# Loading w4 by seven and wo by two neighbouring rows per partition, with w3, V and the gather's operand read in steps

## The chip, the cores and the metric

One core of a Trainium2 chip runs the whole program. Its engines are TensorE (PE; loads of the stationary operand are listed apart as PEld), VectorE (DVE), ScalarE (ACT), GpSimd (POOL) and SyncE (SP), which issues nearly all transfers; 16 DMA engines carry them. The metric is device time in microseconds (us), the median of several runs.

## The reference

Two layers, each an attention block and an MLP block, for eight rows (one token each) of width 448, in bf16:

```
x = x + A(layernorm(x));  x = x + B(layernorm(x));  x = x + A(layernorm(x));  x = x + B(layernorm(x))

A(x): q = x @ wq                       16 heads of 256; 8 K/V heads, each shared by two q heads
      p = softmax(q . k_cache / 16)    over 4096 cached positions per row and K/V head
      o = p . v_cache
      return o @ wo                    wo is 4096 x 448: row 256*head + d

B(x): (x is one token: the shifted branch of the reference adds zeros)
      h = gelu(layernorm(x) @ w3)      w3 is 448 x 1792
      return x + h @ w4                w4 is 1792 x 448
```

Both layers use the same weights and the same caches. k_cache and v_cache are 8 x 8 x 4096 x 256 bf16, 134 MB each. The kernel keeps some K between the layers and loads V twice.

## The kernel before, in words

**Tiles.** A K or V head of one row is 2 MB, cut into four blocks of 512 KB; a block fills one of 31 slots in SBUF (`slots`, `NSLOT`), 2048 bf16 on each of 128 partitions, which is eight neighbouring cache positions of 256. One transfer brings one, two or four blocks. wq, wo, w3 and w4 stay in SBUF. wo lies as 32 tiles of 128 rows x 448 (`wo_sb`), w4 as 14 such tiles (`w4_sb`): partition m of tile t holds row 128 t + m, so that a transfer takes 448 elements (896 B) at a time from DRAM. w3 lies with its 448 input features on partitions, as three tiles and a rest (`w3_sb`, `w3t_sb`).

**Attention.** K blocks are turned for the scores either by TensorE and ScalarE (`transpose`, evicted by a copy) or by VectorE in 32 x 32 squares (line 960, which writes to another slot). TensorE forms the scores (lines 948, 969, 997). For V there are two forms, in `vpart`:

- *still* (line 1111): a 128 x 128 piece of a V block is the stationary operand, and two columns of probabilities move. The output has the head's 256 features on partitions, as two columns `cc` of 128. A block takes 16 matmuls.
- otherwise (line 1137): the probabilities are stationary and V moves, 512 columns at a time. The sum over partitions of the result follows in `gather` (line 1159): ScalarE and VectorE copy the sum from PSUM into a slot as two bf16 parts, and pieces of 128 columns of it are the stationary operand of eight matmuls.

Both leave the attention output with 128 features of a head per column; `outproj` (1185) and `outproj8` (1200) multiply such a column with the wo tile of the same 128 features.

**The MLP.** `project` multiplies 128 columns of w3 (stationary) with the normed token, 14 times four matmuls (lines 588 and 590), into 14 columns of PSUM; `gelu` works on these; `down` multiplies column k with w4's tile k (line 613). All eight batch rows together pass through it once at the end (`end`), and each row alone passes between its two layers, in a *turn* (`turn`, `block`): output projection, norm, w3, gelu, w4, norm, and wq for layer 1. The last row passes the last MLP alone as well (`end1`). In `block` w3's product runs beside the reciprocal root of the norm's variance (lines 545 to 555 on VectorE, after a sum over partitions on GpSimd), and both meet in the scaling at line 675.

**Order.** `Plan.schedule` is a list scheduler that runs before the launch. It books each operation at a given cost and each transfer at its bytes divided by 410 (or 415) bytes per ns, one after the other. From this it settles the order of instructions on every engine, the slot of each block, and whether a transfer of two or four blocks is cut. SP issues the transfers in that order, each as soon as its slots are free. The byte counts of wo and w4 carry a factor of 1.1 in these bookings. wo's transfers are issued after ten transfers of the first K and V blocks, w4's after the first row's layer-0 blocks.

The loads of w3, wo and w4, before (lines 440, 449 and 450 of the kernel):

```
U_w3 = [rows(f"w3{k}", w3_sb[:, k, :], B_w3[k * P:(k + 1) * P, :], P * 3584) for k in range(3)]
...
U_wo = [rows(f"wo{i}", wo_sb[:, 8 * i:8 * i + 8, :], wo_src[:, 8 * i:8 * i + 8, :], P * 7168 * 1.1) for i in range(4)]
U_w4 = [rows("w4", w4_sb[:, :, :], B_w4.rearrange("(t m) n -> m t n", m=P), P * 12544 * 1.1)]
```

Of the kernel before, what the change touches and what calls it, by code (L numbers as in the profile page):

```python
# [3 lines left out]
P = 128  # L4
# [5 lines left out]
DH = 256  # L10
F = 1792
NCH = 4
# [348 lines left out]
def bass_interleave_layers__gqa_block_cached__mixer_s_mlp__decode_kernel(  # L361
# [83 lines left out]
        u.side = True  # L445
    U_even = [U_wq.pop(), U_w3.pop()]
    wq_rest, w3_rest = ([U_side[i], U_even[i]] for i in range(2))
    wo_src = A_wo.rearrange("(t m) n -> m t n", m=P)
    U_wo = [rows(f"wo{i}", wo_sb[:, 8 * i:8 * i + 8, :], wo_src[:, 8 * i:8 * i + 8, :], P * 7168 * 1.1) for i in range(4)]
    U_w4 = [rows("w4", w4_sb[:, :, :], B_w4.rearrange("(t m) n -> m t n", m=P), P * 12544 * 1.1)]  # L450

    def chunks(cache, b, h, name, skip=(), most=2):

# [123 lines left out]

        return j // 4 * 4 + j % 2 * 2 + j // 2 % 2

    def project(w, wt, half, j0, j1, rhs, out0, nb, units, bufs, name, place=lambda j: j):  # L580


        def emit(e):
            last = None
            for j in range(j0, j1):
                o = psT[:, out0 + place(j) * nb:out0 + (place(j) + 1) * nb]
                for k in range(3):
                    e.matmul(o, w[:, k, j * P:(j + 1) * P], rhs(0, P, k), start=(k == 0), stop=False)
                i, k = (j, 4) if j < half else (j - half, 3)
                last = e.matmul(o, wt[:, i * P:(i + 1) * P], rhs(0, P, k), start=False, stop=True)  # L590
            return last
        add("pe", emit, (j1 - j0) * 4 * 27, bufs, [], [bT], units, name=name, n=4 * (j1 - j0))

# [60 lines left out]
    def block(b, n, last, base):  # L654


        x = xT[:, :, b]
        dve(lambda e: e.memset(syn, 0.0), 125, [], [Bs["yn"]], name=n + "c0")
        dve(lambda e: e.memset(sx1[64:128, 4:5], 0.0), 125, [], [Bs["x4"]], name=n + "c1")
        dve(lambda e: e.tensor_reduce(sjk[:, :], psT[:, base:base + 24].rearrange("p (s c) -> p c s", c=4), axis=AX.X, op=ALU.add),  # L660
            180, [], [Bs["jk"]], [bT], name=n + "ao")
        dve(lambda e: e.tensor_tensor(sjk[:, :], sjk[:, :], x[:, 0:4], ALU.add), 150, [Bs["jk"], Bx[b]], [Bs["jk"]], name=n + "xa")
        outproj(*last, [0], base)
        dve(lambda e: e.tensor_tensor(sjk[:, :], psT[:, base + 24:base + 28], sjk[:, :], ALU.add), 150, [Bs["jk"]], [Bs["jk"]], [bT], name=n + "xb")
        plan.turn = not base
        outproj(*last, [1], base)
        dve(lambda e: e.tensor_tensor(sx1[:, 0:4], psT[:, base + 28:base + 32], sjk[:, :], ALU.add), 150, [Bs["jk"]], [Bs["x1"]], [bT], name=n + "x1")
        norm1(sx1[:, :], Bs["x1"], Bs["x4"], 40, n + "a")
        rhs = lambda p0, p1, k: syn[p0:p1, k, 1:2]
        project(w3_sb, w3t_sb, 7, 0, 14, rhs, 16, 1, U_w3 + w3_rest, [Bs["yn"]], n + "w3")  # L670
        root(lambda: sf[:, 5:6], lambda k: sf[:, (1, 6, 7, 8)[k]:(2, 7, 8, 9)[k]],
             (WEIGHT[0] / WEIGHT[1], WEIGHT[0] * (EPS[0] - EPS[1]), ALU.mult, ALU.add), [Bs["sq"]], [Bs["f1"]], [], n + "n1", True)
        dve(lambda e: e.scalar_tensor_tensor(sxy[:, :], sxc[:, 0:4], sf[:, 5:6], sx1[:, 0:4], ALU.mult, ALU.add),
            160, [Bs["xc"], Bs["f1"], Bs["x1"]], [Bs["xy"]], name=n + "xy")
        gelu(1, lambda: shf[:, :], lambda: sht[:, :], 16, [], n, 150, lambda e, o, i: e.tensor_single_scalar(o, i, sf[:, 2:3], ALU.mult), Bs["f"])
        down(1, lambda: sht[:, :], 32, [], n + "w4")
        dve(lambda e: e.scalar_tensor_tensor(x[:, 0:4], psT[:, 32:36], 0.5, sxy[:, :], ALU.mult, ALU.add), 150,
            [Bs["xy"]], [Bx[b]], [bT], name=n + "r2")
# [114 lines left out]
    def end():  # L793

        w = Wide(None, wq_sb[:, 0, 0:SLOT])
        u = []
        v3 = lambda a: a.rearrange("p (c b) -> p c b", b=B)
        x1, x3 = w.tile(bf, 40), w.tile(bf, 32)
        b1, by, b3 = Buf(), Buf(), Buf()
        ao, xy = w.tile(f32, 32), w.tile(f32, 32)  # L800
        bao = Buf()
        b1.readers = [r for u_ in U_wq for r in u_.readers]
        dve(lambda e: e.memset(x1()[64:128, 32:40], 0.0), 100, [], [b1], units=u, name="ex0")
        for m in range(HKV // 2):
            outproj8(m, m, plan.prio)
        dve(lambda e: e.tensor_reduce(ao(), psT[:, 0:256].rearrange("p (s c) -> p c s", c=32), axis=AX.X, op=ALU.add),
            450, [], [bao], [bT], units=u, name="eao")
        dve(lambda e: e.tensor_tensor(x1()[:, 0:32], ao(), xT[:, 0:4, :].rearrange("p c b -> p (c b)"), ALU.add), 200, [bao, b1] + Bx, [b1], units=u, name="ex1")
        u_, bu, yn, byn, roots = norm8(w, lambda: v3(x1()), [b1], 320, "e")
        rhs = lambda p0, p1, k: yn()[p0:p1, 8 * k:8 * k + 8]  # L810
        project(w3_sb, w3t_sb, 7, 0, 14, rhs, 32, 8, U_w3 + w3_rest + u, [byn], "ew3")
        mul, br = roots(True, "e")
        mul1, br1 = roots(False, "ey")
        dve(lambda e: mul1(e, xy(), u_()[:, 0:32]), 200, [bu, br1], [by], units=u, name="ey")
        dve(lambda e: e.tensor_tensor(xy(), xy(), x1()[:, 0:32], ALU.add), 200, [by, b1], [by], units=u, name="exy")
        ht, hf = w.tile(bf, 112), w.tile(f32, 112)
        Bg = {k: Buf() for k in ("ht", "hf")}
        gelu(8, hf, ht, 32, u, "e", 280, mul, br, Bg)
        down(8, ht, 160, u, "ew4", Bg)
        dve(lambda e: e.scalar_tensor_tensor(x3(), psT[:, 160:192], 0.5, xy(), ALU.mult, ALU.add), 200, [by], [b3], [bT], units=u, name="er2")  # L820

        def back(e):
            last = None
            for cc in (3, 0, 1, 2):
                d0 = cc * P if cc < 3 else D - P
                o = psT[0:B, 0:224].bitcast(bf)[:, d0:d0 + P]
                last = e.transpose(o, x3()[:, 8 * cc:8 * cc + 8], ident[:, :])
            return last
        add("pe", back, 400, [b3, Bc], [], [bT], u, name="eback")
        xo = w.tile(bf, D)  # L830
        bxo = Buf()
        dve(lambda e: e.tensor_copy(xo()[0:B, :], psT[0:B, 0:224].bitcast(bf)), 450, [], [bxo], [bT], units=u, name="exo")
        late.append(plan.load(Unit("out", lambda e, _: e.dma_start(out[0:B - 1, 0, :], xo()[0:B - 1, :]), 7168, slotted=False),
                              after=bxo.writers))
        return w
# [244 lines left out]
    def vpart(at, p, still, bank, most, aside):  # L1080
# [14 lines left out]
        if still:  # L1095
            for s in range(2):
                x = bank ^ s if layer else bank
                for c in range(NCH):
                    u = p.V[NCH * s + c]

                    def pv(e, u=u, c=c, s=s, x=x):

                        for cc in range(2):
                            o = psV[x][:, 4 * s + 2 * cc:4 * s + 2 * cc + 2]
                            for j in range(8):
                                i = j * DH + cc * P
                                if c < p.nns[s]:
                                    w = apart(pN[z] if own_(s, c) else pT[y])[:, j // 2, c, 2 * (j % 2):2 * (j % 2) + 2, s]
                                else:
                                    w = apart(pT[y])[:, j % 4, p.place(s, c), 2 * (j // 4):2 * (j // 4) + 2, s]  # L1110
                                last = e.matmul(o, slots[u.slot][:, i:i + P], w, start=(c == 0 and cc == 0 and j == 0), stop=(c == NCH - 1 and cc == 1 and j == 7))  # L1111
                        return last
                    o = add("pe", pv, 430, Bp(s, c), [], [bV[x]], [u], prio=at + 0.02 * (NCH * s + c), name=f"{n}V{s}{c}", n=16)
                    if c:
                        o.deps[first] = True
                    else:
                        first = o
# [3 lines left out]
        else:  # L1121
# [32 lines left out]
            def gather(e):  # L1154
                for cc in range(2):
                    for k in range(4):
                        i = DH * (k % 2) + P * cc
                        w = same[:, 0:8].rearrange("p (s k h) -> p k s h", s=2, k=2)[:, k % 2]
                        last = e.matmul(to[:, 4 * cc:4 * cc + 4].rearrange("p (s h) -> p s h", s=2), part(k // 2)[:, i:i + P], w,  # L1159
                                        start=(k == 0), stop=(k == 3))  # L1160
                return last
            add("pe", gather, 300, Bhalf + [Bsel], [], [bank], [v], prio=at - 1, name=n + "vg", n=8)
# [125 lines left out]
    for b in range(B):  # L1288
# [5 lines left out]
        n = b + 1  # L1294
# [162 lines left out]
```

## Time and profile before

| | |
|---|---|
| median of 3 runs | 1092.66 us (1092.45 to 1092.69) |
| the profiled execution | 1093.51 us, its span 1091.6 us |
| busy in the span | PE 769.7 us (71%), DVE 833.1 (76%), ACT 212.5 (19%), POOL 72.0 (7%) |
| mean granted TensorE clock | 0.603 |
| DMA | 448.96 MB, mean 411 GB/s; the loads' queue busy 98.5% |
| transfers | wo 4 of 896 KB, w4 one of 1568 KB |

Busy times are those of one execution under the profiler; a busy PE counts matmuls that overlap. A span is measured from the first to the last instruction, and the execution's time is some 2 us longer. A share of DMA near 1 says that all 16 engines have a packet in work, not that the packets move at full rate: the rate stands beside it.

### The profile page before, as it was taken

The page shows a single profiled execution, that of the slowest core. Times are in us where ns is not written, and L with a number is a line of the kernel's source. Part 1 is how long each engine was busy: PE and PEld are TensorE (multiplying, and loading weights), DVE is VectorE, ACT ScalarE, POOL GpSimd, SP SyncE. Part 2 cuts the span into 40 slices and gives each one's busy share as a digit, 9 for nine tenths or more (in the row PEclk, how much of TensorE's full clock was granted, in tenths as well). Part 3 has the DMA queues.
Part 4 walks back from the last instruction along what each step waited for, and adds up shares of the span by engine and source line. Part 5 has one row for each costly group of instructions (what it writes and reads, how often), then busy time and mean ns, then how long its engine had stood idle before and what let it go on. Part 6 is the DMA issues. An engine that isn't in the chain of part 4 may idle for free.

```text
span 1091.6 us, 33778 instructions
## 1 busy us (share of the span) xinstructions
PE 769.7 (71%) x15440; PEld 522.0 (48%) x15440; DVE 833.1 (76%) x1597; ACT 212.5 (19%) x323; POOL 72.0 (7%) x233
## 2 busy tenths in 40 slices
PE   2466585778576966768667787578766796666877
PEld 2255453465246633565325654365433654446545
DVE  4999559965996499954999569974799839996483
ACT  1022130213011311203112032121221221111300
POOL 0000000000000000000000010000100001000000
PEclk9998566556655655555655565555665555555665
DMA  9999999999999999999999999999999999999995
GB/s 360 406 421 418 410 419 424 422 409 419 428 422 402 415 428 426 423 390 421 427 426 420 392 424 428 426 417 401 425 428 424 412 404 427 425 423 405 401 425 230
DMA packets 54991, 448.96 MB, mean 411 GB/s; under 512 B 5552, under 2 KB 11584, under 8 KB 14656
## 3 DMA queue, kind: packets, MB, share of 16 engines
q1 hardware_dynamic: 54688, 446.42, 98.5%
q8 instruction: 121, 1.98, 0.7%
q10 hardware_dynamic: 160, 0.38, 0.1%
q14 instruction: 22, 0.18, 0.0%
HBM read 446.77 MB, written 0.01 MB: 409 GB/s over the span
## 4 chain that ended last, share of the span: by engine, by line
DMA 34%; DVE 32%; PE 21%; issue 6%; SPq 4%; ACT 2%; POOL 0%; POOLq 0%; DVEq 0%
DVE slots L960 25%; DMA slots<-in_A_k_cache_dram 22%; DMA slots<-in_A_v_cache_dram 12%; PE psV L1137 6%; PE psS L969 4%; SPq L434 3%; DVE pT L1067 2%; PE psV L1111 1%; ACT slots L938 1%; PE psT L702 1%; PE psT L613 1%; PE psS L948 1%; DVE slots L1150 1%; SPq L459 1%; PE psK L878 1%
## 5 line engine op out<-in xcount | busy, mean ns | idle before, releaser
L960 DVE STREAM_TRANSPOSE slots<-slots 128x1024 bf16<-128x1024 bf16 x544 | 647.9, 1228 | 35.5 <-DMA slots<-in_A_k_cache_dram 27.9
L969 PE MATMUL psS<-qe,slots 128*128 128x8 bf16 x5760 | 225.1, 174 | 160.3 <-DVE slots L960 112.8
L969 PEld LDWEIGHTS psS<-qe,slots 128*128 128x128 bf16 x5760 | 190.8, 103 | 249.4 <-DVE slots L960 180.1
L1137 PE MATMUL psV<-slots,pT 128*8 128x512 bf16 x1528 | 186.3, 565 | 21.7 <-DMA slots<-in_A_v_cache_dram 15.9
L938 ACT COPY slots<-psK 128x1024 bf16<-128x1024 bf16 x80 | 78.4, 1015 | 164.3 <-PE psK L878 152.3
L878 PE MATMUL psK<-ident,slots 128*128 128x128 bf16 x640 | 74.7, 303 | 2.7 <-DMA slots<-in_A_k_cache_dram 2.3
L1031 POOL PARTITION_ALL_REDUCE small<-small x64 | 23.8, 372 | 719.8 <-DVE small L1029 466.8
L1148 ACT ACTIVATE slots<-psV 128x512 bf16<-128x512 f32 x48 | 28.7, 597 | 206.8 <-PE psV L1137 206.8
L878 PEld LDWEIGHTS psK<-ident,slots 128*128 128x128 bf16 x640 | 62.4, 140 | 7.5 <-issue 3.9
L997 PE MATMUL psS<-slots,qe 128*8 128x512 bf16 x232 | 56.0, 605 | 9.0 <-DVE slots L960 7.1
L1137 PEld LDWEIGHTS psV<-slots,pT 128*8 128x8 bf16 x1528 | 31.0, 90 | 53.5 <-DMA slots<-in_A_v_cache_dram 20.6
L1111 PE MATMUL psV<-pT,slots 128*128 128x2 bf16 x1568 | 50.7, 165 | 6.6 <-DMA slots<-in_A_v_cache_dram 5.6
L1111 PEld LDWEIGHTS psV<-pT,slots 128*128 128x128 bf16 x1568 | 47.3, 104 | 8.7 <-DMA slots<-in_A_v_cache_dram 6.3
L1067 DVE STREAM_TRANSPOSE pT<-psS 128x128 bf16<-128x128 bf16 x64 | 45.3, 707 | 5.7 <-PE psS L1059 3.0
L1052 ACT ACTIVATE pT<-psS 128x128 bf16<-128x128 f32 x56 | 15.5, 277 | 172.3 <-DVE psS L1049 172.1
L1150 DVE TENSOR_TENSOR slots<-psV,slots 128x512 bf16<-128x512 f32 x48 | 32.5, 676 | 20.5 <-ACT slots L1148 20.4
L1185 PE MATMUL psT<-small,wo_sb 128*128 128x1 bf16 x1024 | 35.1, 166 | 7.3 <-DVE small L1118 5.3
L1159 PE MATMUL psV<-same,slots 128*128 128x4 bf16 x320 | 14.3, 166 | 35.7 <-DVE slots L1150 30.7
L948 PE MATMUL psS<-qo,slots 128*128 128x2 bf16 x768 | 27.9, 167 | 14.8 <-ACT slots L938 10.3
L1185 PEld LDWEIGHTS psT<-small,wo_sb 128*128 128x128 bf16 x1024 | 32.2, 104 | 9.5 <-DVE small L1118 6.6
L638 DVE TENSOR_TENSOR qe<-psT,small 128x32 bf16<-128x32 f32 x32 | 5.9, 184 | 40.2 <-PE psS L969 36.7
L948 PEld LDWEIGHTS psS<-qo,slots 128*128 128x128 bf16 x768 | 24.1, 102 | 22.0 <-ACT slots L938 15.7
(195 smaller groups left out, 744.9 us busy)
## 6 DMA issues: line engine op xcount, KB each, us to landing
slots<-in_A_v_cache_dram SPq DMA_DIRECT2D x149, 1024.0 KB, 9.9
slots<-in_A_v_cache_dram SPq DMA_DIRECT2D x49, 2048.0 KB, 22.8
slots<-in_A_k_cache_dram SPq DMA_DIRECT2D x46, 2048.0 KB, 21.4
slots<-in_A_k_cache_dram SPq DMA_DIRECT2D x67, 1024.0 KB, 14.8
slots<-in_A_v_cache_dram SPq DMA_DIRECT2D x18, 512.0 KB, 8.8
wo_sb<-in_A_wo_dram SPq DMA_DIRECT2D x4, 896.0 KB, 19.2
wq_sb<-in_A_wq_dram SPq DMA_DIRECT2D x3, 1024.0 KB, 10.8
w_sb<-in_B_w_dram SPq DMA_DIRECT2D x1, 1568.0 KB, 16.4
```

What stands on the lines that cost most here:

```text
L434: return plan.load(Unit(u, lambda e, u_: e.dma_start(t, ap), nbytes, slotted=False))
L878: last = e.transpose(tile[:, j * P:(j + 1) * P], slots[u.slot][:, o:o + P], ident[:, :])
L938: return e.copy(slots[u.slot][:, 1024 * t:1024 * t + 1024], tile)
L948: last = e.matmul(o, slots[u.slot][:, i:i + P], q, start=(cc == 0), stop=(cc == 1))
L960: return e.transpose(o, i)
L969: last = e.matmul(o, slots[u.slot][:, i:i + P], qe[:, 128 * k + 64 * s + 8 * g:128 * k + 64 * s + 8 * g + 8], start=(g == 0), stop=(g == 7))
L997: last = e.matmul(o, q, K[:, lo:hi + 1:hi - lo, :, g, :], start=(g == 0), stop=(g == 7))
L1067: add("dve", lambda e: e.transpose(pZ[:, :, 0:3:2].rearrange("p n s r -> p n r s"), psS[x][:, 128:192].bitcast(bf).rearrange("p (n r s) -> ...
L1111: last = e.matmul(o, slots[u.slot][:, i:i + P], w, start=(c == 0 and cc == 0 and j == 0), stop=(c == NCH - 1 and cc == 1 and j == 7))
L1137: last = e.matmul(psV[x][32 * i:32 * i + 8, :].rearrange("p (k d) -> p k d", k=2), w, v, start=(s == 0 and c == 0), stop=(s == 1 and c == ...
L1150: add("dve", lambda e: e.tensor_tensor(part(1), psV[x][:, :], part(0), ALU.subtract), 590, [Bhalf[0]], [Bhalf[1]], [bV[x]], [v], prio=at - ...
L1185: last = e.matmul(psT[:, base + 4 * (2 * s + i) + c:base + 4 * (2 * s + i) + c + 1], wo_sb[:, a, d0:d0 + P], qo[:, a, b:b + 1] if base els ...
```

## The change

- wo is loaded so that partition m holds rows 2m and 2m + 1 of a head's 256: one run of 1792 B instead of two of 896 B in different places. Tile 2 h + c now has rows 256 h + 2 m + c.
- w4 is loaded in two halves of 896 rows, partition m holding seven neighbouring rows of each: runs of 6272 B. Tile 7 h + t has rows 896 h + 7 m + t.
- For the features of a tile to agree, the stationary operands that make them are read in steps: every seventh column of w3 (`project` with `step=7`; wq's product keeps step 1), and every second column of V (the *still* form) and of the gather's operand.
- In the planner the factors on wo's and w4's bytes fall from 1.1 to 1.05 and 1.02.

```diff
-    wo_src = A_wo.rearrange("(t m) n -> m t n", m=P)
-    U_wo = [rows(f"wo{i}", wo_sb[:, 8 * i:8 * i + 8, :], wo_src[:, 8 * i:8 * i + 8, :], P * 7168 * 1.1) for i in range(4)]
-    U_w4 = [rows("w4", w4_sb[:, :, :], B_w4.rearrange("(t m) n -> m t n", m=P), P * 12544 * 1.1)]
+    wo_src = A_wo.rearrange("(h m c) n -> m h (c n)", m=P, c=2)
+    U_wo = [rows(f"wo{i}", wo_sb[:, 8 * i:8 * i + 8, :].rearrange("p (h c) n -> p h (c n)", c=2), wo_src[:, 4 * i:4 * i + 4, :], P * 7168 * 1.05) for i in range(4)]
+    U_w4 = [rows("w4", w4_sb[:, :, :].rearrange("p (h t) n -> p h (t n)", h=2), B_w4.rearrange("(h m t) n -> m h (t n)", h=2, t=7), P * 12544 * 1.02)]
...
-    def project(w, wt, half, j0, j1, rhs, out0, nb, units, bufs, name, place=lambda j: j):
+    def project(w, wt, half, j0, j1, rhs, out0, nb, units, bufs, name, place=lambda j: j, step=1):
...
+                i, k4 = (j, 4) if j < half else (j - half, 3)
+                c0, n = (i * P, P) if step == 1 else (i, half * P - i)
                 for k in range(3):
-                    e.matmul(o, w[:, k, j * P:(j + 1) * P], rhs(0, P, k), start=(k == 0), stop=False)
-                i, k = (j, 4) if j < half else (j - half, 3)
-                last = e.matmul(o, wt[:, i * P:(i + 1) * P], rhs(0, P, k), start=False, stop=True)
+                    e.matmul(o, w[:, k, (j - i) * P + c0:(j - i) * P + c0 + n:step], rhs(0, P, k), start=(k == 0), stop=False)
+                last = e.matmul(o, wt[:, c0:c0 + n:step], rhs(0, P, k4), start=False, stop=True)
...
-        project(w3_sb, w3t_sb, 7, 0, 14, rhs, 16, 1, U_w3 + w3_rest, [Bs["yn"]], n + "w3")
+        project(w3_sb, w3t_sb, 7, 0, 14, rhs, 16, 1, U_w3 + w3_rest, [Bs["yn"]], n + "w3", step=7)
...
-                                i = j * DH + cc * P
+                                i = j * DH + cc
...
-                                last = e.matmul(o, slots[u.slot][:, i:i + P], w, start=(c == 0 and cc == 0 and j == 0), stop=(c == NCH - 1 and cc == 1 and j == 7))
+                                last = e.matmul(o, slots[u.slot][:, i:i + DH - cc:2], w, start=(c == 0 and cc == 0 and j == 0), stop=(c == NCH - 1 and cc == 1 and j == 7))
...
-                        i = DH * (k % 2) + P * cc
+                        i = DH * (k % 2) + cc
...
-                        last = e.matmul(to[:, 4 * cc:4 * cc + 4].rearrange("p (s h) -> p s h", s=2), part(k // 2)[:, i:i + P], w,
+                        last = e.matmul(to[:, 4 * cc:4 * cc + 4].rearrange("p (s h) -> p s h", s=2), part(k // 2)[:, i:i + DH - cc:2], w,
                                         start=(k == 0), stop=(k == 3))
```

More of the change, by code (lines that the diff above doesn't have):

```diff
@@ L810, in end @@
         rhs = lambda p0, p1, k: yn()[p0:p1, 8 * k:8 * k + 8]
-        project(w3_sb, w3t_sb, 7, 0, 14, rhs, 32, 8, U_w3 + w3_rest + u, [byn], "ew3")
+        project(w3_sb, w3t_sb, 7, 0, 14, rhs, 32, 8, U_w3 + w3_rest + u, [byn], "ew3", step=7)
         mul, br = roots(True, "e")
```

## The prediction

> **What bounds the kernel now.** I read the page first, then tables of busy time by stretch, the chain of waits, the timeline of the last 20 us, and the instructions that use w3 and w4.
>
> From the page, rates in 40 slices of 27.3 us and the packet count:
>
> ```profile
> DMA  9999999999999999999999999999999999999995
> GB/s 360 406 421 418 410 419 424 422 409 419 428 422 402 415 428 426 423 390 421 427 426 420 392 424 428 426 417 401 425 428 424 412 404 427 425 423 405 401 425 230
> DMA packets 54991, 448.96 MB, mean 411 GB/s; under 512 B 5552, under 2 KB 11584, under 8 KB 14656
> ```
>
> The loads run from the first slice to the last. 6032 packets lie between 512 B and 2 KB; wo and w4 account for 4096 + 1792 = 5888 of them (one row of 448 bf16, 896 B, each). But "busy" doesn't mean full rate, so I cut the span by stage (columns: stretch, its us, busy us of PE, PEld, DVE, ACT, POOL, granted clock, DMA share, GB/s):
>
> ```profile
> 37.00:48.00 11.00, 6.37 (x97) 2.96 (x97) 10.86 (x13) 0.59 (x2) 0.74 (x3) 1.00 1.07 379
> 115.00:120.00 5.00, 2.79 (x93) 2.66 (x94) 5.00 (x8) 0.12 (x1) 0.00 (x0) 0.50 1.06 384
> 381.00:469.00 88.00, 59.66 (x1001) 36.87 (x999) 82.31 (x113) 15.68 (x25) 5.77 (x19) 0.52 1.01 425
> 469.00:491.00 22.00, 15.13 (x392) 13.22 (x391) 9.85 (x32) 2.20 (x3) 1.61 (x5) 0.50 0.97 384
> 491.00:513.00 22.00, 20.74 (x439) 12.12 (x435) 9.69 (x44) 8.53 (x12) 1.34 (x4) 0.58 1.01 418
> ```
>
> The first two are the stretches in which wo's and w4's rows move: 379 and 384 GB/s against 425 in a steady stretch. The fourth is the 22 us ahead of a turn (batch row 3's single-token chain: wo, w3, w4, wq), 384; the fifth the turn itself, 418. So the DMA bounds nearly everything, and it loses most ahead of the turns: 22 x (1 - rate/425), with 404, 391, 384, 387, 395, 391 and 378 GB/s in front of the last seven, is 1.1, 1.8, 2.1, 2.0, 1.6, 1.8 and 2.4 us, 12.8 in all. There SP waits for slots that V holds: between 470 and 492 us its longest waits are on PE's L1111, 12.6 us in six.
>
> The chain of waits at its end (start, us, what):
>
> ```profile
> 1085.45 0.07 DVE small L553
> 1085.52 0.12 DVE small L552
> 1085.65 0.07 DVE small L554
> 1085.72 0.12 DVE small L553
> 1085.84 0.08 DVE small L555
> 1085.92 0.04 issue
> 1085.96 0.23 DVE qe L675
> ```
>
> After the last V block lands, a chain of small steps ends the span. Here w3's product (PE) and the root (VectorE) run side by side and meet at L675. The timeline has w3's last matmul start at 1085.54 and last 0.17: it is done at 1085.71, and L675 starts at 1085.96. The root is what ends last, w3 has 0.25 us to spare.
>
> **The change, part by part.**
>
> *Fewer rows per transfer.* wo: 4096 packets of 896 B become 2048 of 1792 B; w4: 1792 become 256 of 6272 B. wo is 4 x 896 KB = 3.67 MB: 9.68 us at 379 GB/s, 8.64 at 425, 1.04 to gain at most. w4 is 1568 KB = 1.61 MB: 4.18 us at 384, 3.78 at 425, 0.40 at most. If the loss is a fixed time per packet, wo loses half of it and w4 six sevenths: 0.52 + 0.34 = 0.86 us. Bounds 0.86 and 1.44; I take 0.9, since a fixed cost per packet is what is left in the neighbouring rates (425 isn't reached everywhere). At the low end stands 0 if the stages behind, paced by slots, do not pass it on; in the steady stretches the DMA never waits, so I let it pass.
>
> *SP.* The four wo issues hold SP from 14.01 us for 28.66 (one of them 17.5), as the queue is full. With half the packets SP comes free earlier, but the DMA share there is 1.00 to 1.09: the queue already has work. Nothing gained; without that cover it would be under 1 us, once.
>
> *w3 in steps of seven.* Count and shape stay: 56 weight loads and 56 matmuls per product, nine single ones and one for eight rows. Now 56 loads of L613 (w4, the same shape, packed) take 1.57 us in the tail with 0.10 for one: (1.57 - 0.10)/55 = 26.7 ns apart. No load with a step lies in the trace. The nearest row is L531, whose weights are one column read 128 times: four loads in 0.18 to 0.19 us, so (0.185 - 0.104)/3 = 27 ns apart, the same. Bounds: 0, and a doubled spacing, 56 x 26.7 = 1.50 us. (A gain is excluded: a step can't be read faster than the packed row.) I take 0 from L531. The cover is the root: up to 0.25 us, or 4.5 ns per load, is free in the tail, some 0.3 in six of eight turns, nothing in the other two (L675 waited 0.25 us for w3 at 623 and 885 us). Behind L675 wait gelu, w4, the second norm, wq's rows and the scores that free K's slots.
>
> [...]
>
> *V in steps of two.* 2048 loads (L1111, 64 groups of 32). Bounds 0 and doubled, 16 x 26.7 = 0.43 us per 512 KB block. Blocks arrive 1.25 us apart at the end (L1111 starts at 1077.79 and 1079.06), a block's matmuls take 0.59, so only the last one's growth would show there; ahead of a turn, where its slot is what SP waits for, each one might. I take 0 by the same row. *The gather* (L1159, 48 groups of 8 loads, 0.35 us): at most 8 x 26.7 = 0.21 us each; in the tail it ends before the next V block has landed. 0.
>
> *The planner.* Its transfer times fall: wo 4 x 128 x 7168 x 0.05 / 410 = 0.45 us, w4 128 x 12544 x 0.08 / 410 = 0.31. Everything it books later lands 0.76 us sooner by its account, so it may order the engines' work and choose slots otherwise, from 14 us on. No row prices that. The nearest: the seven stretches ahead of turns do the same work in orders of their own and lose 1.1 to 2.4 us each. All at the best would be 12.8 - 7 x 1.1 = 5.1 us faster, all at the worst 7 x 2.4 - 12.8 = 4.0 slower; drawn anew, about 0.45 x sqrt(7) = 1.2 either way. I take 0.
>
> Sum: the profiled execution, 1093.51 us (span 1091.6 and 1.9 around it), less 0.9 is 1092.6. The median of the runs, 1092.66, lies 0.85 below the profiled one; on it the sum is 1091.8.
>
> **The rivals.** A difference of 0.2%, 2.2 us, is about what a measurement of this kernel can tell from none: faster is below 1090.5, slower above 1094.8.
>
> 1. *The forecast*: 0.9 us off the DMA, steps free, order much the same: 1091.8, between 1090.5 and 1093.0. For it: steady 425 GB/s, w3's slack, L531. Chance 0.42.
>
> 2. *Slower: w3's stepped loads at half pace.* The place is L675, the price 1.50 less the slack, 1.25 us, from 4.5 ns per load on. In the tail all of it shows: 1092.66 - 0.9 + 1.25 = 1093.0. In each of eight turns the freeing of slots comes 1.25 to 1.5 us later. The turns now run at 418 to 420 GB/s, so there is queue left, but the stage ahead of them at 384 shows how thin it is; a third of 8 x 1.25 passed on gives 3.3: 1096.3. All of it would be 1103. For: nothing in the trace reads weights with a step. Against: the turns' rate. Chance 0.28, four in five of it above 1094.8.
>
> 3. *Slower: V's stepped loads.* Doubled, each 512 KB block holds its slot 0.43 us longer; its loop is about 9.9 us (the page's median from issue to landing), so 4% of 22 us, 0.9, seven times, and 0.43 at the end: 1092.66 - 0.9 + 6.3 + 0.4 = 1098.5. Chance 0.07.
>
> 4. *The planner's order decides*: 1091.8 with 1.2 to 5 less (1087 to 1090.5) or 1.2 to 4 more (to 1096). That the losses ahead of turns differ twofold speaks for it; that all its bookings move by one amount speaks against. Faster 0.15, slower 0.08.
>
> That the change does nothing, because the 0.9 us is lost in the slot-bound stages, gives 1092.7 and lies within the first.
>
> **The numbers.** Faster: 0.15 from the order and 0.04 of the forecast (the 1.44 with a lucky order), 0.19. Slower: 0.22 + 0.07 + 0.08 + 0.02 of the forecast, 0.39. Same: 0.36 + 0.06, 0.42. The range: down to 1088.5 (order better by some 3), up to 1098.5 (half-pace loads with half of the delay in the turns, or the third rival). Left out are about 0.06 below and 0.12 above. The forecast's own range is 1090.5 to 1093.0.
>
> **What would show it.** Right: no stretch at 379 or 384 GB/s around 40 and 117 us, under 2 KB some 3840 packets fewer; L588 and L590 still 27 ns apart and L675 released by the root; stretches ahead of turns at 378 to 404 in the same order. Wrong: w3's 56 loads taking 2 us or more and L675 waiting for L590 (rival 2); L1111's groups of 32 over 1.2 us (rival 3); other waits of SP and other pairs of 512 KB and 1 MB loads with unchanged PE times (rival 4).

## The result, and the profile after

The changed kernel takes 1097.56 us (median of 6 runs, 1096.17 to 1099.17) beside 1092.76 for the kernel before: ratio 1.0040, 95% interval 1.0029 to 1.0050, so 3.2 to 5.5 us slower. The forecast was 1091.8 and "about the same"; the time lies in the stated range, at the price of its second rival. The profiled execution took 1097.53 us with a span of 1095.7, against 1093.51 and 1091.6.

In the file after, the lines of `project` are 592 and 593 (588 and 590 before), L675 is L678, L1111 is L1114 and L1159 is L1162.

From the page of the kernel after, the packets:

```profile
DMA packets 51407, 448.96 MB, mean 410 GB/s; under 512 B 5552, under 2 KB 7744, under 8 KB 11072
```

Under 2 KB there are 11584 - 7744 = 3840 packets fewer, as counted beforehand. By stage (the columns as in the table before: stretch, its us, PE, PEld, DVE, ACT, POOL, granted clock, DMA share, GB/s):

```profile
40.00:46.00 6.00, 4.64 (x64) 1.77 (x64) 5.86 (x6) 0.00 (x0) 0.00 (x0) 1.00 1.06 381
116.00:121.00 5.00, 3.69 (x123) 3.48 (x124) 5.00 (x8) 0.00 (x0) 0.00 (x0) 0.67 1.04 429
...
469.00:491.00 22.00, 15.54 (x378) 13.62 (x379) 10.95 (x28) 2.20 (x3) 1.24 (x5) 0.58 0.99 389
491.00:513.00 22.00, 21.04 (x456) 13.69 (x455) 9.52 (x49) 8.53 (x12) 1.72 (x5) 0.66 1.00 414
```

Before, the first of these stretches, in which wo's rows move, was

```profile
40.00:46.00 6.00, 4.25 (x56) 1.47 (x56) 5.86 (x8) 0.31 (x1) 0.24 (x1) 1.00 1.10 382
```

w4's stretch (115 to 120 us before) went from 384 to 429 GB/s. wo's did not move: 382 before, 381 after. So half as many packets, twice as long, bought nothing for wo. The 22 us ahead of the fourth turn (469 to 491) and the turn itself (491 to 513) run at 389 and 414 GB/s, where they ran at 384 and 418.

The instructions that use w3 (duration in ns, min/median/max), from the answer on the tile:

```profile
L592 PEld LDWEIGHTS psT<-qe,w_sb x378: 131/154/154, 136.0 to 1089.7; 128*128 128x128 bf16 x189
L592 PE MATMUL psT<-qe,w_sb x378: 163/192/213, 136.0 to 1089.7; 128*128 128x1 bf16 x189
L616 PEld LDWEIGHTS psT<-qe,w_sb x504: 103/104/118, 140.4 to 1092.7; 128*128 128x128 bf16 x168
```

Before, the first of these lines was

```profile
L588 PEld LDWEIGHTS psT<-qe,w_sb x378: 102/104/117, 136.7 to 1085.5; 128*128 128x128 bf16 x189
```

A load of w3 in steps of seven takes 154 ns, where a packed one took 104. More telling is the distance between loads. The chain of waits at its end (start, us, what):

```profile
1086.80 0.32 PE psT L592 x3
1087.12 0.05 PE psT L593
1087.17 0.16 PE psT L592 x3
1087.33 0.05 PE psT L593
...
1089.89 0.07 PE psT L593
1089.96 0.03 issue
...
1090.01 0.05 issue
1090.05 0.23 DVE qe L678
```

Four matmuls come every 0.21 us: 53 ns each, where it was 26.7. And the chain now runs through PE's w3 up to L678; before, it ran through VectorE's root. What L678 waits for, by the answer on its line:

```profile
L678 DVE TENSOR_SCALAR qe<-psT,small x9: 231/232/233, 139.2 to 1090.1; 128x14 bf16<-128x14 f32 x9
its engine sat idle before it (us, times) until:
  PE psT L593: 11.1, 9
```

It waits in all nine single-token products, 11.1 us together. L675 before waited twice, 0.5 us in all:

```profile
  PE psT L590: 0.5, 2
```

V's steps of two show nothing (the answer on the costliest groups; busy, mean ns of one):

```profile
L1114 PEld LDWEIGHTS psV<-pT,slots 128*128 128x128 bf16 x1568 | 47.3, 104 | 7.5 <-DMA slots<-in_A_v_cache_dram 5.5 <-issue 1.8
L1162 PEld LDWEIGHTS psV<-same,slots 128*128 128x128 bf16 x320 | 11.9, 103 | 47.1 <-issue 39.0 <-ACT slots L941 4.2 <-ACT slots L1151 3.5
```

Before, V's loads had the same 104 ns and the same 47.3 us (L1111). The distance between them is unchanged as well, by the trace: 27 ns at the median, before and after, for V and for the gather.

### The profile page after: what moved, and what is told of

It is laid out like the page before. It is cut to its first block, busy times and chain, and to the rows that moved or that the text cites. A ratio compares the mean times of both kernels' runs of the same rounds, so it can differ in the third digit from the quotient of the medians.

```text
span 1095.7 us, 33778 instructions
## 1 busy us (share of the span) xinstructions
PE 780.9 (71%) x15440; PEld 536.6 (49%) x15440; DVE 833.7 (76%) x1597; ACT 212.4 (19%) x323; POOL 72.4 (7%) x233
## 2 busy tenths in 40 slices
DMA packets 51407, 448.96 MB, mean 410 GB/s; under 512 B 5552, under 2 KB 7744, under 8 KB 11072
## 4 chain that ended last, share of the span: by engine, by line
DVE 33%; DMA 28%; PE 27%; issue 5%; ACT 4%; SPq 3%; POOL 0%; DVEq 0%
DVE slots L963 26%; DMA slots<-in_A_k_cache_dram 17%; DMA slots<-in_A_v_cache_dram 10%; PE psV L1140 7%; PE psS L972 6%; SPq L434 3%; PE psT L592 2%; DVE pT L1070 2%; PE psS L951 2%; ACT slots L941 2%; PE psV L1114 1%; PE psT L616 1%; PE psT L705 1%; DVE slots L1153 1%; SPq L461 1%
## 5 line engine op out<-in xcount | busy, mean ns | idle before, releaser
L1114 PE MATMUL psV<-pT,slots 128*128 128x2 bf16 x1568 | 50.7, 165 | 5.4 <-DMA slots<-in_A_v_cache_dram 4.8
L1114 PEld LDWEIGHTS psV<-pT,slots 128*128 128x128 bf16 x1568 | 47.3, 104 | 7.5 <-DMA slots<-in_A_v_cache_dram 5.5
L1162 PE MATMUL psV<-same,slots 128*128 128x4 bf16 x320 | 14.3, 166 | 38.2 <-DVE slots L1153 32.2
L1162 PEld LDWEIGHTS psV<-same,slots 128*128 128x128 bf16 x320 | 11.9, 103 | 47.1 <-issue 39.0
## 6 DMA issues: line engine op xcount, KB each, us to landing
slots<-in_A_k_cache_dram SPq DMA_DIRECT2D x67, 1024.0 KB, 15.3
```

The source lines that it names most:

```text
L1114: last = e.matmul(o, slots[u.slot][:, i:i + DH - cc:2], w, start=(c == 0 and cc == 0 and j == 0), stop=(c == NCH - 1 and cc == 1 and j == 7))
```

## The experiments

The theory after the result: w3's loads in steps of seven are the loss, in the tail and in each turn (theory 1). Rivals: V's and the gather's steps (2), the long rows themselves (3). The fourth rival of the prediction falls: with the factors 1.05 and 1.02 the planner gives the same program as with 1.1, instruction for instruction, slots and waits included. In the traces, too, every engine and SP go through the same sequence of operations before and after, and all kernels here share one order but for the instructions named with each.

**w3 packed again, the rest of the change kept.**

```diff
-        project(w3_sb, w3t_sb, 7, 0, 14, rhs, 16, 1, U_w3 + w3_rest, [Bs["yn"]], n + "w3", step=7)
+        project(w3_sb, w3t_sb, 7, 0, 14, rhs, 16, 1, U_w3 + w3_rest, [Bs["yn"]], n + "w3")
...
-        project(w3_sb, w3t_sb, 7, 0, 14, rhs, 32, 8, U_w3 + w3_rest + u, [byn], "ew3", step=7)
+        project(w3_sb, w3t_sb, 7, 0, 14, rhs, 32, 8, U_w3 + w3_rest + u, [byn], "ew3")
```

> The changed kernel with w3 read in packed columns again (long rows of w4 and wo and V's and the gather's steps stay; w3's features then no longer agree with w4's rows, so the output is not the reference's). If w3's loads in steps of seven are the whole loss (theory 1), the time falls to the forecast's sum, 1091.8 us, and w3's 56 loads stand 27 ns apart again. If V's or the gather's steps carry a part (theory 2), it stays above 1093 by that part. If the long rows themselves slow the stream (theory 3), it stays at 1094 to 1097.

Measured: 1092.33 us, 0.9990 of before (0.9980 to 1.0000). All of the loss is gone. The loss is w3's steps; V's steps and the rows have no part that shows.

**Only the long rows.** The kernel before, with after's three lines of `wo_src`, `U_wo` and `U_w4` (factors 1.1), nothing in steps.

> The kernel before with only the long rows of wo and w4 and the changed bytes of their transfers; w3, V and the gather are read packed (features do not agree, so the output is not the reference's). The planned order is that of before. If the saving of 0.9 us in the early transfers reaches the end, 1091.8 us; if the slot-bound stages ahead of the turns eat it, 1092.7; if the long rows cost something, over 1093. The difference to the kernel with V's steps is the price of these alone: theory 1 says 0, theory 2 says 1 to 6 us.

Measured: 1092.77 us, 0.9994 (0.9983 to 1.0005). The interval holds both 0 and the saving of 0.9 us; with the kernel above the ratio is 0.9990. The rates say 0.4 us for w4 and nothing for wo; the times can't tell.

**Only w3 in steps of seven**: on the kernel before, the reverse of that diff, with after's `project`.

> The kernel before with only w3 read in steps of seven (rows of w4 and wo as before, so the features do not agree and the output is not the reference's). Theory 1: the whole loss and no saving, 1097.6 + 0.9 = 1098.5 us, with w3's product taking 2.97 us in every turn and the rates behind the turns at 400 to 414 GB/s. If V's steps or the rows carry the loss: 1094 at most, the 1.25 us of the tail.

Measured: 1098.27 us, 1.0043 (1.0029 to 1.0056): 4.7 us. The step alone makes the loss.

**Steps 1 to 7 side by side.**

```diff
-                c0, n = (i * P, P) if step == 1 else (i, half * P - i)
+                c0, n, st = (i * P, P, 1) if step == 1 else (0, 127 * (i + 1) + 1, i + 1)
```

> The kernel before, where w3's product reads tile j and j + 7 in steps of j + 1, so steps 1 to 7 stand side by side in each product (other columns of w3 than the reference's, so the output differs). [...] The time of the whole, by theory 1: with three of seven tiles slow, 3/7 of the 1.42 us per product, 0.6 us, of which 0.3 is covered in most turns: 1093 to 1094.5 us.

The timeline of PEld in the tail's product: start, duration of a group, line. Each tile is three loads of w3 and one of its rest; tiles 1 to 7 follow each other with steps 1 to 7:

```profile
1085.49 0.16 PEld L590 LDWEIGHTS psT<-qe,w_sb 128*128 128x128 bf16 x3
...
1085.59 0.16 PEld L590 LDWEIGHTS psT<-qe,w_sb 128*128 128x128 bf16 x3
...
1085.70 0.18 PEld L590 LDWEIGHTS psT<-qe,w_sb 128*128 128x128 bf16 x3
...
1085.83 0.20 PEld L590 LDWEIGHTS psT<-qe,w_sb 128*128 128x128 bf16 x3
...
1085.98 0.23 PEld L590 LDWEIGHTS psT<-qe,w_sb 128*128 128x128 bf16 x3
...
1086.16 0.26 PEld L590 LDWEIGHTS psT<-qe,w_sb 128*128 128x128 bf16 x3
...
1086.37 0.19 PEld L590 LDWEIGHTS psT<-qe,w_sb 128*128 128x128 bf16 x3
```

The starts are those of steps 2 to 7 and, last, of step 1 again. From one to the next a tile of four takes 0.10, 0.11, 0.13, 0.15, 0.18 and 0.21 us: by the trace, medians of 27 ns per load up to step 3, then 33, 40, 47 and 54 ns for 4, 5, 6 and 7. The expectation's sum takes three slow tiles of seven; four are slow, those from step 4 on. The one time, 1095.25 us, lies 2 us above before, but a single run cannot carry that.

**Steps of seven in the tail alone, and in the turns alone**, otherwise the changed kernel:

```diff
-        project(w3_sb, w3t_sb, 7, 0, 14, rhs, 16, 1, U_w3 + w3_rest, [Bs["yn"]], n + "w3", step=7)
+        project(w3_sb, w3t_sb, 7, 0, 14, rhs, 16, 1, U_w3 + w3_rest, [Bs["yn"]], n + "w3", step=7 if base else 1)
```

This is the tail (`base` is 0 in a turn); the other has `step=1 if base else 7`. Both read w3 packed in `end`.

> The changed kernel with w3 read in steps of seven only in the last row's own MLP at the end, packed in the eight turns and in the product for all rows (features agree only there, so the output is not the reference's). The profile gives the tail 1.2 us (w3's product 2.97 us instead of 1.55, 0.25 of it beside the root), on 1092.3 us of the kernel with all of w3 packed: 1093.5. If the delay in the tail were the whole loss, 1097; if it were hidden, 1092.3.

> The counterpart: steps of seven only in the eight turns, packed in the tail and for all rows (again the output is not the reference's). If the turns' later freeing of slots is the larger part (theory 1), 1092.3 plus the remaining 3 to 4 us: 1095.5 to 1096.3. If slots cover the turns, 1092.3.

Measured: 1093.99 us (1.0009 of before, 1.0001 to 1.0018) and 1095.80 (1.0024, 1.0013 to 1.0035). Over the median of the kernel with all of w3 packed (1092.33) that is 1.7 and 3.5 us, together 5.1 (unrounded), and the changed kernel stands 5.2 above it. By the ratios to the kernel before, which stand on runs of the same chip, it is 2.1 and 3.7 against 5.5. Each part is known to about a microsecond, so that the sum comes out this closely is luck. Both parts are there, the turns are the larger one, and nothing clear is left for the product of all eight rows, which is packed in both. What L678 waits for in each:

```profile
  PE psT L593: 1.3, 1
```

in the tail alone, where it adds 1.3 us to the chain and 1.7 to the time, and

```profile
  PE psT L593: 8.5, 8
```

in the turns alone, of which about 3.5 reach the end, four tenths.

How a turn passes it on shows in the rates. With w3 packed, the 22 us from the start of w3's product, for the second, fourth and seventh turn:

```profile
247.00:269.00 22.00, 19.93 (x482) 12.89 (x479) 10.38 (x52) 8.52 (x12) 1.73 (x5) 0.73 1.01 420
489.00:511.00 22.00, 20.00 (x478) 12.91 (x475) 9.94 (x51) 8.53 (x12) 1.74 (x5) 0.73 1.01 419
882.00:904.00 22.00, 19.67 (x478) 12.78 (x475) 9.88 (x49) 8.53 (x12) 1.53 (x5) 0.73 1.00 417
```

and the same in the changed kernel:

```profile
248.00:270.00 22.00, 20.76 (x428) 13.09 (x425) 8.77 (x44) 8.53 (x12) 1.34 (x4) 0.66 0.99 398
491.00:513.00 22.00, 21.04 (x456) 13.69 (x455) 9.52 (x49) 8.53 (x12) 1.72 (x5) 0.66 1.00 414
884.00:906.00 22.00, 21.52 (x437) 13.36 (x434) 8.71 (x47) 8.53 (x12) 1.67 (x5) 0.58 1.01 415
```

Over all eight turns the mean is 416 GB/s packed (414, 420, 412, 419, 413, 419, 417, 417) and 409 in steps (399, 398, 411, 414, 413, 413, 415, 412): 8 x 22 x (1 - 409/416) = 3.0 us of transfer lost. The kernel before has 419 over its eight turns, which would make it 4.2, so this estimate holds to about a microsecond. The last V block lands at 1084.2 us instead of 1081.3, by the trace, 2.9 later. These are single executions; over all traces it lands at 1080.0 to 1081.5 where the turns read w3 packed, and at 1082.8, 1084.2 and 1086.0 in the three kernels whose turns read it in steps of seven.

**Only V's and the gather's steps of two**, on the kernel before:

```diff
-                                i = j * DH + cc * P
+                                i = j * DH + cc
...
-                                last = e.matmul(o, slots[u.slot][:, i:i + P], w, start=(c == 0 and cc == 0 and j == 0), stop=(c == NCH - 1 and cc == 1 and j == 7))
+                                last = e.matmul(o, slots[u.slot][:, i:i + DH - cc:2], w, start=(c == 0 and cc == 0 and j == 0), stop=(c == NCH - 1 and cc == 1 and j == 7))
```

The gather is changed in the same way.

> The kernel before with only V (in the still form) and the gather's operand read in steps of two (wo's rows as before, so the features do not agree and the output is not the reference's). Loads 27 ns apart in the changed kernel's trace: no difference, 1092.5 to 1093.2 beside the kernel before. If the steps hold slots longer ahead of the turns, over 1094.

Measured: 1093.74 us, 1.0005 (0.9992 to 1.0018). No loss that can be measured; with 27 ns between loads, as before, there is none to look for.

**w4 by three, two and two rows.**

```diff
+    for h in range(2):
+        for t0, c, r0, k in ((0, 3, 0, 1), (3, 2, 384, 2)):
+            U_w4.append(rows(f"w4{h}{t0}", w4_sb[:, 7 * h + t0:7 * h + t0 + c * k, :].rearrange("p (a c) n -> p a (c n)", c=c),
+                             w4_h[h, r0:r0 + P * c * k, :].rearrange("(a m c) n -> m a (c n)", m=P, c=c), P * 896 * c * k * 1.05))
...
+                c0, st = (i * P, 1) if step == 1 else (i, 3) if i < 3 else (384 + i - 3, 2) if i < 5 else (640 + i - 5, 2)
```

> A version with no step over three: each half of w4 (896 rows) by three, two and two neighbouring rows on a partition (runs of 2688 and 1792 B, four transfers), w3 read in steps of three and two, wo and V as in the changed kernel. All features agree. Steps one to three keep 27 ns, so no turn is longer: 1092.0 to 1092.8, like the kernel with w3 packed; if runs of 1792 B move no faster than 896 B, nearer the upper end. If four transfers instead of one disturb SP's order, above 1093.5.

Measured: 1092.82 us, 0.9995 (0.9986 to 1.0004). The loss is mended (loads of w3 at 104 ns, L678's counterpart waits 0.1 us in all), but it can't be told from the kernel before: there is too little to gain. Its w4 shows something else, in a stretch that is nine tenths runs of 1792 and 2688 B, mixed:

```profile
117.50:120.00 2.50, 1.34 (x45) 1.18 (x43) 2.50 (x5) 0.00 (x0) 0.00 (x0) 0.59 1.04 407
```

407 GB/s, while wo's runs of 1792 B move at 381 in this kernel too. A packet of 1792 B of w4 takes 74 ns, one of wo 79 (means, by the trace). So it seems that the length of a run is not all that sets wo's rate.

**w3's product made long in another way.** Packed columns, each matmul two or three times:

```diff
+                for _ in range(2 if half == 7 and nb == 1 else 1):
                     for k in range(3):
                         e.matmul(o, w[:, k, j * P:(j + 1) * P], rhs(0, P, k), start=(k == 0), stop=False)
```

> The kernel before (packed columns, rows as before) with each of the 56 matmuls of w3's single-token products issued twice, the second pass starting the sum anew, so the product takes 112 loads of 27 ns, 2.97 us, as long as 56 loads of 53 ns. If the length of the product is what costs (theory 1), the same as the kernel before with steps of seven alone: 1097.5 to 1098.5 us. If reading SBUF in steps of seven disturbs other engines or the transfers besides, this one stays well below that, at 1094 (the tail's 1.25 us).

> The same with three passes: 168 loads, some 4.45 us, 2.9 us longer than before in each of eight turns and the tail. The tail then gives 2.65 us. If the turns pass on a third of the delay, 8 x 2.65 / 3 = 7.1: 1102.5 us. If the slots' cover is used up by the first delay, all of what is added beyond passes on: 8 x 1.5 more than with two passes, 1109 to 1111.

Measured: 1106.63 us (1.0124, 1.0106 to 1.0141) and 1124.61 (1.0286, 1.0270 to 1.0302), far above either expectation. As a control this failed: the instructions added are not free. The timeline of PEld in the second turn of the first:

```profile
252.84 0.10 PEld L589 LDWEIGHTS psT<-qe,w_sb 128*128 128x128 bf16 x1
254.49 0.13 PEld L589 LDWEIGHTS psT<-qe,w_sb 128*128 128x128 bf16 x2 [1.55 <-issue]
```

In the midst of the product PE waits for nothing that the profile shows and still stands for 1.55 us. What held it is not shown (the page counts 125 packets of instructions instead of 121). So the products took 3.0 to 4.6 us from the first matmul to the last, and 4.5 to 7.1 with three passes. What remains of use is the wait that resulted, below. Whether stepped reads disturb anything else is not shown by it; that the kernel with steps of seven alone is the faster one (1098.27) speaks against.

**w3 in steps of five**, on the kernel before (`step=5`, columns i to i + 635):

> The kernel before with w3 read in steps of five (other columns than the reference's, so the output differs): 56 loads 40 ns apart, 2.24 us instead of 1.50, so L675 comes 0.5 us later in the tail and 0.45 later in each turn. If each turn has a cover of about half a microsecond and passes on what is beyond it, only the tail shows: 0.5 us over the kernel before on the same chip, 1093.0 to 1093.5. If a turn passes on a fixed share of any delay (0.45, by the kernel with steps of seven alone), 8 x 0.45 x 0.45 = 1.6 us more: 1094.6 to 1095.1.

Measured: 1094.52 us, 1.0018 (1.0002 to 1.0033). That is 2.0 us by the ratio, near the second expectation (2.1 more than before), but the interval of 0.2 to 3.6 holds the first (0.5) as well. Setting the kernels side by side, with the total wait of the scaling (L675 and its counterparts) for w3, and the time added by the ratio:

| w3's product | wait for it, us | time added, us (interval) |
|---|---|---|
| packed (before) | 0.5 | 0 |
| steps of five | 3.6 | 2.0 (0.2 to 3.6) |
| steps of seven alone | 9.8 | 4.7 (3.2 to 6.1) |
| twice | 15.3 | 13.5 (11.6 to 15.4) |
| three times | 36.2 | 31.2 (29.5 to 33.0) |

Roughly half of the wait reaches the end where it is 0.4 to 1.1 us per product, and nearly nine tenths where it is 1.7 to 4.0. A cover of half a microsecond per turn would give 5.8 us in the third row (the waits there are 1.0 us in seven turns, 1.5 in one and 1.3 in the tail), and little but the tail's 0.5 in the second, near the low end there; a fixed share would give 1.6 to 2. The last two rows also contain pauses whose cause is not shown: ahead of w3's matmuls PE stood still, with no wait that the profile shows, for 4.5 and 11.6 us there, and for 1.7 before. The form of the cover stays open.

## Why the prediction was wrong

- *The step that failed* is the price of w3's loads in steps of seven. "I take 0 from L531" used a row in which one column is read 128 times (27 ns from load to load); that row stays at one address, so it could not speak for a step that moves on. The right value was the upper end, 1.50 us per product: from the first matmul to the last, 2.96 us were measured against 1.49.
- *The doubled spacing* was the author's estimate, and no run ahead of the result showed it; nor does any run show the three slow tiles of seven in the expectation for steps 1 to 7. What the runs showed instead: 53 ns from load to load in steps of seven against 27 packed, and side by side 27 ns up to step 3, then 33, 40, 47 and 54 ns, so four slow tiles, and none faster than packed. They show how the price grows with the step, not the reason.
- *The second rival's own working held.* Tail 1.25 us (the wait there 1.3, the time 1.7); a third of the turns' delay, 3.3 us (about 3.5 measured). The third had no row behind it, so that it fits is luck in part; the waits in the turns were 1.0 us in most, less than the 1.25 to 1.5 that it took. Its sum of 1096.3 includes the 0.9 us saved, most of which isn't there; 1097.56 was measured. Its chance, 0.28, was too small for what was known: the unknown cost had no row of its own, and of its two bounds the cheaper one was taken.
- *The cover of 0.25 us* by the root was read rightly for the tail, and so was what ends the chain once it is gone. In the turns the cover is more than the 0.3 taken: 1.47 us of growth leave a wait of 1.0.
- *The rows*: w4's term was right (0.34 taken; the stretch went from 384 to 429 GB/s, 4.18 to 3.74 us, 0.4; these stretches hold rows of w3 as well, but over 110 to 124 us, with all of w4, the rate goes from 405 to 418, 0.4 again). wo's 0.52 was wrong: 381 GB/s in runs of 1792 B as in runs of 896 B. A fixed cost per packet is not what slows these: by the trace one takes 41 ns at 896 B and 79 at 1792 (means). That a saving reaches the end is neither shown nor excluded (0.9994, 0.9983 to 1.0005).
- *SP, V and the gather*: 0 each, as taken. wo's four issues hold SP for 25.45 us, where it was 28.66, with a DMA share of 1.01 and 1.02 meanwhile; that a full queue holds it is the author's reading, and the traces don't show it.
- *The planner*: no change of order at all, so 0.23 of the chances stood on a case that the planner's own output could have ruled out.

## What to carry to other kernels

When a layout is changed so that transfers run longer, look at who reads the tile next: here a stationary operand read in steps of four to seven bf16 was loaded more slowly (33 to 54 ns from load to load against 27, twice at seven), while steps of two and three were free (27 ns). A short product on a latency chain is priced by the wait at its meeting point with the parallel branch, here once for the tail (1.3 us of wait, 1.7 of time) and once for every turn (8.5 us of wait in eight, about 3.5 of time; with all of w3 in steps the turns ran at 409 GB/s instead of 416). For a bound without a row of its own, the nearest row must share the property in question (here: a new place in memory for each weight), or the upper end deserves the better chance.

## What the runs showed of the hardware

- Distance between 128-column bf16 weight loads on PE by the step between columns: 27 ns for steps 1, 2 and 3, then 33, 40, 47 and 54 ns for 4, 5, 6 and 7, some 6.7 ns per further element. The granted clock made no difference to it: nearly all products with w3 ran at 0.50, but in the kernel with steps of seven in the turns alone the first one ran at 1.00 (seventh column) and its 56 loads stand 53 ns apart all the same, and packed loads of wq in the first product stand 27 ns apart at 1.00 as well.

```profile
137.70:140.80 3.10, 3.00 (x56) 3.03 (x56) 1.32 (x12) 0.00 (x0) 0.40 (x1) 1.00 0.97 394
```

- Rates of transfers from DRAM by the length of their runs, in half microseconds or more that hold almost nothing else: about 380 GB/s at 896 B (wo and w4) and at 1792 B (wo), 400 to 410 at 3584 B (w3's own rows), about 430 at 6272 B (w4). The doubling for wo gave nothing, while w4's runs of 1792 and 2688 B together moved at 407. What holds wo back is open; it wasn't tried.
- With 504 matmuls more, in a program of 15440, PE stood still for 1.55 us at one place in the middle of a packed product, with no wait that the profile shows. The stepped product shows less of such pauses: before, three of the nine products took 2.1 to 2.2 us from the first matmul to the last instead of 1.49; in steps of seven, eight take 2.93 to 2.96 and one 3.10.
